# A planned attention and FFN kernel: denominator scaled to a constant of 1, clip free to run on GpSimd, new recorded order

## The chip, the cores and the metric

The kernel runs on one core of one Trainium2 chip. The metric is device microseconds of one execution. The three runs of the kernel before took 618.22, 619.12 and 624.07 us; the median is 619.12 us.

## The reference, cut to what matters

The first half is a gated linear recurrence over 768 time steps for 4 batches and 8 heads of 48 channels. The second half is an FFN of width 2048 whose activation is a rational function.

```python
mag = np.sqrt(a_re * a_re + a_im * a_im)
scale = np.minimum(mag, 0.999) / (mag + 1e-06)          # the clip
for t in range(S):                                       # S_re, S_im: complex 48 x 48 state of each head
    new_re = ar * S_re - ai * S_im
    new_im = ar * S_im + ai * S_re
    S_re, S_im = (new_re + kv, new_im)
    y[:, :, t] = np.einsum('bhd,bhde->bhe', q[:, :, t], S_re)
h = x @ w_in                                             # x: 3072 x 384, w_in: 384 x 2048
P = a[0] + a[1] * h + a[2] * h2 + a[3] * h3
Q = 1.0 + np.abs(b[0]) * np.abs(h) + np.abs(b[1]) * h2   # the denominator
g = P / (Q + 1e-06)
return (g @ w_out).astype(np.float32)
```

## The kernel before, in words

The recurrence is computed in chunks of 128 time steps. A unit is one chunk of one batch; there are 24 units, and two units make a pair (12 pairs). For each unit `norm` squares and clips the gates, takes reciprocal square roots and runs a running product along time; `angle` and `trig` give the phase as a sine and a cosine; `outer` turns q and k by them and copies the result by six DMAs into the buffer HQ; `attn` runs the matmuls of the unit on TensorE: transposes (line 566), scores (line 579, two groups of four heads, each into one of two PSUM banks), the masked scores and the state times the values (line 599), and the state update (line 604). For every pair `ffn` then runs 8 steps of 512 columns. One step is two slices of the hidden width: the first matmul into `ph` (line 632), a chain of elementwise operations, and the second matmul into `po` (line 649). The first two pairs use whole float32 weights, and the other ten pairs use weights and activations split into a high and a low part, so that three cheaper products stand for one. `weights` builds the float32 weights at the start from the raw words that are loaded, and `split` makes the two parts.

The elementwise chain of a step, by engine: ScalarE (ACT) takes |h| from `ph` into A1 and a square with a bias into A3; squares A1 with a bias into A2; takes the reciprocal square root of A2 plus a constant into the PSUM tile `z`; and squares `z`. VectorE (DVE) multiplies `ph` into A3, then makes two steps that refine the reciprocal in `z`, and the product that becomes `g`; in the split pairs `g` is also cut into two parts by ACT or DVE and by DVE or GpSimd (POOL). There are 96 steps.

```python
scal(AF.Square, 512, t2, t1, (A1, "co"), (A2,), more=93, bias=bh)         # line 677
scal(ROOT, 512, tz, t2, (A2, "co"), (z,), bias=q0, more=93)               # line 680, q0 = ks, a column
stt(512, t2, t2, q0, tz, (A2, z, "co"), (A2,))                            # line 682
```

No scheduler of the compiler sets the order. Every operation is put into a plan with the engines that may run it and an estimate of its time. The string ORDER holds a recorded order of all operations and the engine of each, and the operations are issued in that order, so each engine works its own part of the list in turn. The estimates in the plan play no part in an execution as long as ORDER fits the list.

SyncE (SP) issues nearly all DMAs in the same recorded order, and a DMA that waits for its data holds back the ones behind it.

Of the kernel before, what the change touches and what calls it, by code (L numbers as in the profile page):

```python
# [217 lines left out]
def act(n, psum=False):  # L218
# [11 lines left out]
    "=L&f?mR=^o2K7;K+$OfS4wqEwa9LYPDz)3IpUFa^eN(E)My(aH;lV@BT%Ar9s!KIXZ)*{Cw3=z$yb)YIubsrt^hud6F}hO*uv>$$%!0D=FP$vq)yi5O!TpVO"  # L230
    "f;+(8*8nvrR1HQr_cY2R+X?cRv9^qcI9C4`Y$CVhez1~rCwO1Vhz1I6c}Xx+ZIs@XzXOwOs-y(Q*hbDkU81)nUe`*lJ|tswxm*h-)m)VIrT(ci<pVR{-qZR{"
    "QSeZ(hV!nb%Dv!dSuZI}*+cS~+|)14t6mkykx}$yu%<~k8Qj&n&gDSaykxy;zOiLwgjr>;>wCd$NtfYz!)&l2QcF7M5-BUK%|1KasCPp*Nl#PJt|zNO+Fte$"
    "$pEb?bE*6|ljD8Cv}FZa=MA8Djhxa>a_|eLb`AG@PCY->4!Tf2mhw(&@T9hoW6Z@OiF6hO2HHgZf?XHLn`XV;8>}ELo#VmBop_xupOIr4J$gr~OK**KyXVab"
    "&f)q){oIVO2|V?boB=iUWsFSJzd^uh-5{@P2%TvH(ms(z`Ums3QVvT~Enq@cyOX`Yw7mPCjdF$uM>uPODeQ97d}vEclB&*=Bf*%Eq~IIW+tAC}5-%0pA)X^O"
    "Wf)ae9qH88Nm{|Z<V}~yq`y`N%hRN?4w21r(%kTpOl_Ma{iUTg)8E;5r)~_^4XLC3iRqk%$$xYJ75obXzAT$T;KQ=VUF4<nyf8r<xuZZ|W7iJgqPp9Y?ylq6"
    "P-bL~zD=x|ZbR>FDJ4;$_Eo83itGVc<6Dzs6SNdqE~2uf<tVe7s=FkS3igtCceVG0CNn{f>@UG%ruLBy+EAJidnZtKP<Odwy>(RZS=pldLC0!6F5R@BOk=f6"
    ";A|PY>~^nuPit>^1U{%E&&Uqb&wc`af~;Ar#l-%a+u!R*T_)=oNpw4TF<f6`*FD-*o^tznBe>d2oi=)VV3dh)$4{n{y{l>TY?u3kcUOypKTDi!(huE%u*?{F"
# [713 lines left out]
```

## Time and profile before

| | |
|---|---|
| median of three runs | 619.12 us |
| the profiled execution: its time, and the span from first to last instruction | 621.97 us, 620.2 us |
| TensorE (PE) busy | 552.5 us, 89% of the span |
| VectorE (DVE) busy | 561.2 us, 90% |
| ScalarE (ACT) busy | 515.7 us, 83% |
| GpSimd (POOL) busy | 278.9 us, 45% |
| mean granted TensorE clock | 0.984 of full speed |

The profile is one execution, and the sums are made against it. Busy time of an engine is the union of its instructions, so two instructions that overlap in the pipeline are counted once; a group's mean duration counts the overlap. Matmul ends are modelled, so a short pause between two matmuls can hide inside a busy TensorE.

### The profile page before, as it was taken

The numbers are of one execution on the slowest core, as the hardware profiler recorded it, in microseconds if no ns is written. First come the engines' busy times: TensorE is split into PE (matmuls) and PEld (weight loads), VectorE is DVE, ScalarE is ACT, GpSimd is POOL, SyncE is SP. The second block draws the span as 40 slices with busy tenths as digits, with TensorE's granted clock in tenths as the row PEclk, the third lists the DMA queues.
The fourth block names the chain that finished last, engine by engine and source line by source line (L and its number), as shares of the span: only waits on it lengthen the run. The fifth ranks groups of instructions, "written<-read, shape, count | busy, mean of one in ns | idle before, by whom it ended". The sixth has DMA issues, their size and how long they took to land.

```text
span 620.2 us, 16732 instructions
## 1 busy us (share of the span) xinstructions
PE 552.5 (89%) x6786; PEld 506.8 (82%) x6786; DVE 561.2 (90%) x984; ACT 515.7 (83%) x886; POOL 278.9 (45%) x244
## 2 busy tenths in 40 slices
PE   0048868899999999999999999899999999999994
PEld 0036645687679999999999999899999999999993
DVE  8999999799999999998999998989899989986893
ACT  7746999789799999999899899789888798677780
POOL 1012452457478587565465885663755400211110
PEclk9999988899999999999999999899999999999998
DMA  8699227474524470461461541553543604130001
GB/s 298 214 255 305 90 77 144 80 144 104 116 57 121 95 158 15 105 163 27 77 175 53 132 97 32 98 127 97 95 113 78 150 2 88 38 102 2 1 1 57
DMA packets 39109, 64.87 MB, mean 105 GB/s; under 512 B 4464, under 2 KB 26224, under 8 KB 39024
## 3 DMA queue, kind: packets, MB, share of 16 engines
q1 hardware_dynamic: 37872, 62.67, 40.6%
q10 hardware_dynamic: 1152, 1.05, 0.9%
q8 instruction: 55, 0.90, 0.7%
q14 instruction: 30, 0.25, 0.1%
HBM read 40.11 MB, written 4.72 MB: 72 GB/s over the span
## 4 chain that ended last, share of the span: by engine, by line
PE 64%; DVE 20%; DMA 7%; ACT 4%; issue 3%; SPq 1%; POOL 0%; ACTq 0%; DVEq 0%; POOLq 0%
PE po L649 26%; PE ph L632 26%; PE bank L599 5%; PE bank L579 4%; DVE A L338 4%; DMA HQ<-Q 3%; DVE T L338 3%; DVE MM L338 2%; PE bank L566 2%; PE bank L604 1%; DVE wo L338 1%; DVE z L338 1%; DVE wi L338 1%; ACT A L350 1%; DMA AA<-in_aa 1%
## 5 line engine op out<-in xcount | busy, mean ns | idle before, releaser
L649 PE MATMUL po<-wh,g 128*128 128x384 f32 x640 | 181.4, 340 | 0.0
L632 PE MATMUL ph<-xT,wiH 128*128 128x256 f32 x960 | 161.7, 287 | 0.3 <-DVE A L338 0.3
L649 PE MATMUL po<-wo,g 128*128 128x384 f32 x428 | 148.2, 387 | 2.1 <-DVE g L338 2.0
L338 DVE SCALAR_TENSOR_TENSOR A<-A,co,z 128x512 f32<-128x512 f32 x176 | 130.5, 742 | 20.1 <-ACT z L350 17.7
L632 PEld LDWEIGHTS ph<-xT,wiH 128*128 128x128 f32 x960 | 136.7, 191 | 2.5 <-DVE A L338 0.7
L632 PE MATMUL ph<-xT,wi 128*128 128x256 f32 x632 | 128.3, 322 | 7.2 <-DVE A L338 4.1
L338 POOL TENSOR_TENSOR g<-A,g 128x512 fp32r<-128x512 f32 x48 | 65.1, 1364 | 137.0 <-ACT z L350 40.2
L649 PEld LDWEIGHTS po<-wh,g 128*128 128x128 f32 x640 | 117.2, 188 | 2.1 <-issue 0.6
L632 PEld LDWEIGHTS ph<-xT,wi 128*128 128x128 f32 x632 | 103.0, 195 | 17.1 <-DVE A L338 4.1
L649 PEld LDWEIGHTS po<-wo,g 128*128 128x128 f32 x428 | 80.4, 191 | 15.1 <-DVE g L338 2.4
L350 ACT ACTIVATE z<-A,co 128x512 f32<-128x512 f32 x96 | 66.3, 690 | 21.8 <-DVE A L338 18.5
L338 DVE SCALAR_TENSOR_TENSOR A<-A,co,ph 128x512 f32<-128x512 f32 x96 | 71.0, 739 | 9.4 <-ACT A L350 9.4
L350 ACT ACTIVATE A<-A,co 128x512 f32<-128x512 f32 x96 | 69.1, 720 | 1.4 <-DVE g L338 0.4
L350 ACT ACTIVATE A<-ph,co 128x512 f32<-128x512 f32 x96 | 65.2, 680 | 3.3 <-DVE A L338 1.7
L338 DVE SCALAR_TENSOR_TENSOR z<-A,z 128x512 f32<-128x512 f32 x96 | 66.3, 691 | 1.8
L350 ACT ACTIVATE A<-ph 128x512 f32<-128x512 f32 x96 | 56.7, 591 | 11.7 <-PE ph L632 9.2
L566 PE MATMUL bank<-ident,HQ 96*128 96x96 f32 x160 | 19.5, 260 | 44.1 <-DVE wh L338 36.2
L350 ACT ACTIVATE z<-z 128x512 f32<-128x512 f32 x96 | 56.2, 585 | 1.5
L566 PEld LDWEIGHTS bank<-ident,HQ 96*128 96x128 f32 x160 | 17.1, 147 | 47.1 <-issue 42.3
L579 PEld LDWEIGHTS bank<-HQ 96*32 96x32 f32 x1536 | 32.8, 117 | 10.3 <-issue 3.0
L338 DVE TENSOR_TENSOR ST<-bank,cmask 128x512 f32<-128x512 f32 x48 | 32.0, 683 | 8.8 <-PE bank L579 8.3
L579 PE MATMUL bank<-HQ 96*32 96x32 f32 (+3 forms) x1536 | 37.8, 248 | 1.4 <-ACT kT L344 1.1
(175 smaller groups left out, 957.7 us busy)
## 6 DMA issues: line engine op xcount, KB each, us to landing
HQ<-Q SPq DMA_DIRECT2D x136, 128.0 KB, 5.1
AA<-in_aa SPq DMA_DIRECT2D x23, 384.0 KB, 3.6
QK<-in_qk SPq DMA_DIRECT2D x23, 384.0 KB, 4.9
V<-in_v SPq DMA_DIRECT2D x24, 352.0 KB, 4.7
g<-in_w_out SPq DMA_DIRECT2D x8, 384.0 KB, 5.2
wh<-in_w_in SPq DMA_DIRECT2D x6, 512.0 KB, 4.3
wh<-in_w_out SPq DMA_DIRECT2D x8, 384.0 KB, 4.3
g<-in_w_in SPq DMA_DIRECT2D x6, 512.0 KB, 5.2
```

Of the source, the lines that this page charges most:

```text
L338: call = lambda e: getattr(e, kind)(*map(real, args), **{k: real(x) for k, x in kw.items()})
L350: plan.op(dict(ACT=(act(n, psum) + more, lambda e: e.activation(o(), i(), f, **kw))), r, w)
L566: e.transpose(pt[:, i].bitcast(F32R), hq[0:96, 4 * g + i, 1, :], ident[0:96, 0:96])
L579: e.matmul(pst[m:m + 32, i, 32 * y:C], hf[:, 4 * g + i, 1, 32 * y:32 * y + 32], hf[:, 4 * g + i, 0, 32 * y:C], start=True, stop=True)
L599: e.matmul(py[32 * y:32 * y + 32, min(j, 2), :], l, sts[h // 4][:, h % 4, :] if q is None else hf[:, h, 0, :], start=q is None and j == 0, ...
L604: e.matmul(pd[y:y + 32, h], kT[:, h, y:y + 32], V[:, n:n + D], start=True, stop=True)
L632: e.matmul(ph[:, x * T:x * T + T].rearrange("p (h t) -> p h t", h=nb), wt[f // 4 * NJ + j][:, f % 4 * P:f % 4 * P + P], xT[:, x0:x0 + nb, ...
L649: e.matmul(po[b][:, 0:DM], gg[:, b * C:b * C + C], wt[:, 0:DM], start=(f == 0 and n == 0), stop=(f == NFF - 1 and n == len(prods) - 1))
```

## The change: what it does, and the diff

A factor `al` is computed once from the coefficients, by the reciprocal square root of the old constant `ks` and one refining step. The square of A1 takes `al` as a scale beside its bias, so that the constant to be added to A2 becomes 1. The reciprocal square root and the first refining step then take the number 1.0 where they took a column of `co`. The clip of `norm` may be placed on DVE or POOL. The string ORDER is another one; its characters are left out below. The estimates of `scores` and `values` in the plan differ, and one threshold in the test of the coefficients.

```diff
 ORDER = (
...
-    ra, rb, c2, c2h, c1, c1s, c0, bh, ks, sc, tmp = (co[:, i:i + 1] for i in range(11))
+    ra, rb, c2, c2h, c1, c1s, c0, bh, ks, sc, tmp, al = (co[:, i:i + 1] for i in range(12))
...
+    def scales(e):
+        e.tensor_tensor(tmp, al, al, ALU.mult)
+        e.tensor_tensor(tmp, tmp, ks, ALU.mult)
+        e.tensor_scalar(tmp, tmp, -0.5, 1.5, ALU.mult, ALU.add)
+        e.tensor_tensor(al, al, tmp, ALU.mult)
+        e.tensor_tensor(bh, bh, al, ALU.mult)
         e.tensor_tensor(sc, av[:, 3:4], rb, ALU.mult)
-        e.tensor_scalar(sc, sc, -1.0, None, ALU.mult)
-
-    plan.op(dict(DVE=(1500, ratios)), ("ab",), ("co",), port=True)
+        e.tensor_tensor(tmp, al, al, ALU.mult)
+        e.scalar_tensor_tensor(sc, sc, -1.0, tmp, ALU.mult, ALU.mult)
+
+    plan.op(dict(DVE=(1200, ratios)), ("ab",), ("co",), port=True)
+    scal(ROOT, 1, lambda: al, lambda: ks, ("co",), ("co",))
+    plan.op(dict(DVE=(700, scales)), ("ab", "co"), ("co",), port=True)
...
-        vec("tensor_scalar", W, lambda: MM.t, lambda: SQ[:, 1], CLIP2, None, ALU.min, two=False, r=(s1,), w=(MM,))
+        vec("tensor_scalar", W, lambda: MM.t, lambda: SQ[:, 1], CLIP2, None, ALU.min, two=False, r=(s1,), w=(MM,), eng=DP)
...
-            pe(565, scores, u.hq, (pst,))
+            pe(584, scores, u.hq, (pst,))
...
-        pe((1980 if c else 1010) + (0 if last else 600), values, (V, *sts, *u.hq, ("St", bb), *(() if last else (kT,))),
+        pe((1769 if c else 885) + (0 if last else 676), values, (V, *sts, *u.hq, ("St", bb), *(() if last else (kT,))),
...
-                scal(AF.Square, 512, t2, t1, (A1, "co"), (A2,), more=93, bias=bh)
-                k1, k0, q0 = c1s, c0, ks
+                scal(AF.Square, 512, t2, t1, (A1, "co"), (A2,), more=186, bias=bh, scale=al)
+                k1, k0, q0 = c1s, c0, 1.0
...
-            scal(ROOT, 512, tz, t2, (A2, "co"), (z,), bias=q0, more=93)
+            scal(ROOT, 512, tz, t2, (A2,), (z,), bias=q0)
...
-            stt(512, t2, t2, q0, tz, (A2, z, "co"), (A2,))
+            stt(512, t2, t2, q0, tz, (A2, z), (A2,), more=0)
```

Where instructions stand is shown at two places. The first is TensorE early in the split FFN, at the scores of the seventh unit (HQ0). `bank0` and `bank1` are the two PSUM banks of the attention, `ph` is the result of the first FFN matmul, `wiH` and `wi` are the high and the low part of its weights. Before, the last two rows of one group of scores, a slice of the FFN and the first row of the other group:

```order
L579 MATMUL bank1_106<-HQ0_92 32x64
L579 MATMUL bank1_106<-HQ0_92 32x32
L632 MATMUL ph_1805<-xT_1536,wiH3_850 128x256
L632 MATMUL ph_1805<-xT_1536,wiH4_1119 128x256
L632 MATMUL ph_1805<-xT_1536,wiH5_737 128x256
L632 MATMUL ph_1805<-xT_1536,wi2_1265 128x256
L632 MATMUL ph_1805<-xT_1536,wi3_1309 128x256
L632 MATMUL ph_1805<-xT_1536,wi4_1315 128x256
L632 MATMUL ph_1805<-xT_1536,wiH3_850 128x256
L632 MATMUL ph_1805<-xT_1536,wiH4_1119 128x256
L632 MATMUL ph_1805<-xT_1536,wiH5_737 128x256
L579 MATMUL bank0_105<-HQ0_92 32x128
```

Now, at the scores of the same unit:

```order
L589 MATMUL bank1_106<-HQ0_92 32x128
L589 MATMUL bank1_106<-HQ0_92 32x96
L589 MATMUL bank1_106<-HQ0_92 32x64
L589 MATMUL bank1_106<-HQ0_92 32x32
L589 MATMUL bank0_105<-HQ0_92 32x128
L589 MATMUL bank0_105<-HQ0_92 32x96
L589 MATMUL bank0_105<-HQ0_92 32x64
L589 MATMUL bank0_105<-HQ0_92 32x32
```

The two groups of scores now follow each other without FFN matmuls between them. Counted over the whole order, other matmuls stand between the two groups in 13 of the 24 units before (the 6th, 7th, 10th, 11th, 14th to 17th, 19th to 23rd) and in 1 now (the 22nd).

The second place is DVE in the first pair's FFN, while the weights are still being built. A row that writes `z` ends one FFN step. `wi` and `wo` are weights being built, `Q` are the turned q and k that the six DMAs of a unit read, `SQ`, `MM`, `T` and `RU` are tiles of `norm` and `outer`. Before, between the fourth and the fifth row that writes `z`:

```order
L338 SCALAR_TENSOR_TENSOR z<-A_747,z 128x512
L338 SCALAR_TENSOR_TENSOR g<-A_744,co,z 128x512
L338 COPY ncar<-MM 128x3
L338 TENSOR_REDUCE fl<-T 128x2
L338 TENSOR_SCALAR MM<-SQ 128x384
L338 SCALAR_TENSOR_TENSOR A_787<-A_787,co,ph 128x512
L338 SCALAR_TENSOR_TENSOR A_771<-A_771,co,z 128x512
L338 SCALAR_TENSOR_TENSOR z<-A_771,z 128x512
```

Now the end of the same piece; seven rows stand ahead of these and behind the fourth row that writes `z`:

```order
L338 SCALAR_TENSOR_TENSOR wo_746<-wh_643,wo_746 128x384
L338 SCALAR_TENSOR_TENSOR MM<-MM,ncar,SQ 128x128
L338 SCALAR_TENSOR_TENSOR RU<-Z,RU 128x3x128
L338 SCALAR_TENSOR_TENSOR MM<-MM,ncar,SQ 128x128
L338 TENSOR_TENSOR RU<-MM,RU 128x3x128
L338 SCALAR_TENSOR_TENSOR MM<-MM,ncar,SQ 128x128
L338 TENSOR_TENSOR T<-T,thc 128x6
L338 TENSOR_TENSOR Q<-QK,CO 128x768
L338 TENSOR_TENSOR Q<-QK,T 128x768
L338 SCALAR_TENSOR_TENSOR A_806<-A_806,z 128x512
L338 SCALAR_TENSOR_TENSOR z<-A_806,z 128x512
```

The piece has 7 rows behind the fourth write of `z` before and 18 now. The two rows that make `Q` of the third unit stand in the fifth step now; before they stand in the seventh. The row that writes A from A and `z` has no `co` any more.

## Rows read from the trace of the kernel before

**Rows 1.** Busy time by stretch: us, busy (instructions) of each engine, granted clock, DMA.

```profile
56.00:172.00 116.00, 102.61 (x970) 76.17 (x971) 109.43 (x199) 100.94 (x174) 56.40 (x51) 0.96 0.51 119
172.00:611.00 439.00, 436.01 (x5511) 418.41 (x5510) 396.40 (x653) 377.62 (x649) 215.49 (x174) 1.00 0.35 81
```

**Rows 2.** The two longest waits of PE, 172 to 612 us: total us, times, longest.

```profile
PE bank L566 <- DMA HQ<-Q: 1.6, 1, 1.6
PE bank L566 <- DVE St L338: 0.9, 2, 0.8
```

**Rows 3.** The chain of waits, in order of time: start us, us, what.

```profile
172.94 2.15 PE ph L632 x18
175.09 1.29 PE po L649 x4
...
216.18 6.47 PE ph L632 x54
...
282.55 1.89 PE bank L599 x64
...
285.11 2.35 PE ph L632 x18
...
288.51 0.61 PE bank L566 x8
...
579.48 3.12 PE po L649 x18
...
599.53 10.94 PE po L649 x63
```

**Rows 4.** Instructions of PE in order of time, scores in one piece: start us, us.

```profile
204.25 0.34 PE L649 MATMUL po<-wh,g 128*128 128x384 f32 x1
204.52 1.33 PE L579 MATMUL bank<-HQ 96*32 96x128 f32 x64
205.78 0.45 PE L649 MATMUL po<-wh,g 128*128 128x384 f32 x1
206.07 0.33 PE L649 MATMUL po<-wo,g 128*128 128x384 f32 x1
```

**Rows 5.** The same view, one group of scores between FFN matmuls.

```profile
243.71 0.52 PE L632 MATMUL ph<-xT,wiH 128*128 128x256 f32 x3
244.15 0.77 PE L579 MATMUL bank<-HQ 96*32 96x128 f32 x32
244.85 0.62 PE L632 MATMUL ph<-xT,wiH 128*128 128x256 f32 x3
245.31 0.52 PE L632 MATMUL ph<-xT,wi 128*128 128x256 f32 x3
```

**Rows 6.** Groups of instructions: count, busy us, mean ns, idle before them.

```profile
L338 DVE SCALAR_TENSOR_TENSOR A<-A,co,z 128x512 f32<-128x512 f32 x176 | 130.5, 742 | 20.1 <-ACT z L350 17.7
L350 ACT ACTIVATE A<-A,co 128x512 f32<-128x512 f32 x96 | 69.1, 720 | 1.4 <-DVE g L338 0.4
L338 DVE SCALAR_TENSOR_TENSOR z<-A,z 128x512 f32<-128x512 f32 x96 | 66.3, 691 | 1.8
L350 ACT ACTIVATE z<-A,co 128x512 f32<-128x512 f32 x96 | 66.3, 690 | 21.8 <-DVE A L338 18.5 <-DVE g L338 1.5 <-DVE T L338 0.8
L692 ACT ACTIVATE g<-A 128x512 fp32r<-128x512 f32 x49 | 30.3, 625 | 2.9 <-PE po L649 2.0 <-DVE A L338 0.9
L338 DVE TENSOR_SCALAR MM<-SQ 128x384 f32<-128x384 f32 x23 | 10.7, 464 | 0.1
L338 POOL TENSOR_SCALAR SQ<-SQ 128x384 f32<-128x384 f32 x3 | 1.6, 522 | 0.0
```

**Rows 7.** Instructions of DVE in order of time, while POOL is idle.

```profile
7.39 0.36 DVE L338 TENSOR_SCALAR MM<-SQ 128x384 f32<-128x384 f32 x1
```

**Rows 8.** Waits of PE and of DVE, 56 to 172 us: total us, times, longest.

```profile
PE bank L566 <- DMA HQ<-Q: 3.0, 1, 3.0
DVE ST L338 <- PE bank L579: 2.8, 2, 2.4
```

More of the change, by code (lines that the diff above doesn't have):

```diff
@@ new lines @@
+    "lH?!#M~zIBdAdhi$v*8UuSr|=q=FRlO)UQgfAS<+Zs{GZDTR7i+UP~CBd0V`3N%bs$|U_=D@p?2#Y%)+(6Z84{?yBQOUp^7Ow-NMTo=h4J;xj8Oon?oQj4wJ"
+    "&;>G1OY|OzmBrFkD@i4JUKVLUf7aC!$#;`wnU0XMQdbVEnkjy)jArLNov%Y|Q#Vr2=u|u1UoVepYw0Xicw>$%;QgcezPzDLWPsc&XW9Rf7HcCptrK(tdAv!?"
+    "lUY})cgq>=9QAGZ%kGv=;k3D0P5Mfr?DgUU6=az??9UYPG!<NZEs`Gki44^$vPIhIE@{Ayec7dw?d!JaOL9=BYjv3<L&)?a?IUrly;}xJRq3U3r4#SGBl-G<"
+    "J|sR-WSUCu3CYsurHL6Y<6OQb$ZdT^zarjVx`IsZlU%JV$zea<sUTCR_*8jZhHFyTkAZ?fr?6djZtCMyVxp|qfm9`$%HIl|pW`jM6Cstndn1pRgh^>2!8;YG"
@@ new lines @@
+    "?3Dy!rMBeBI(<$WnOqkxw|P3=jCGM9psd`Ci7ukV=Bk@vX1Vej<~gmYm*hg=E-zNj2i}&cQeMhwSudUMZ)uFAnu=mwkybZjizX(HIaAMjPM7OHU?E9f(CXe*"
+    "9k16llirr-C>^J>WC0Pz%9)tTZmblURqS%Fbkr=#XLlcr_!^}z*$KY&?qZjb(og4^?(TpLHS^s9A}vF0=S!MdqOnE8^>uv<)C}YEM>zu4K9+rfObO@=T}Yj)"
+    "%TnpA8S<eX)@JepwI8Do*%U{nbb7XorJk`;XeVErDdUN9jUHsp3XP_ZSrX}`1?I^uDNEd*ZRmQjZ)M&bqtl3Xv23JEs;_~V|C*D2yj<3Lbh^4s)MAtGPm<|c"
+    "Uw+q>-V1?-GK7;W$wh4_{lIsBKFflb2_Sr|x#~{?11B{_zZNTlIbp3C;nLZAwLR~z)zjKdv!#sGk`o#ZazE3)62{z316{4837_S~*g<|RdB9}5H`$}5>FHF*"
@@ new lines @@
+    "OOYN3WXm9Lpw^QA1n&1%Yd=|SzIQpM&`*>!%>~z4>{(6@$Y9pwnA?75Spo{X66+x?0K297gACAI?IGJuZ?{}iIqgIKXZhxD{me9Rb-{l+{T(V_>o|!sPrJ97"
+    "!do#5+$jBzyhDW(v<q1u&~186p3!gUYF~K-7T8F|W5~C^UFw&GYi7tu%{2{OroG$$O&U_q2jy?gGSQOa0vg4+&%y|6wJuYUl+^m{2%;ayB)`w3y<k7{-__TN"
+    "<$3vDi@;2=R+X#ztuB{Rv(f*aIvoX#k@RA&US*y?_vdSxybUAW(Cxa?X8HSdfV{4QWRs>4)jrMBAxvFsGI|gkUbIvFoqE~~bgd-b?(*NFzinZhzFNgz@vo7;"
+    "m6v6<egO}Tk)|+Sp}eHQC;y^?LnT8;%RBlLOmLFf{}BE;BX<H7y!~d0AIW*1bhFz+Kcz_vJJb)Cmh}96ovnFNUw6wL6X!PTO`WPonBZ1&*_`ux%0~DogG^Ux"
@@ new lines @@
+    "dHAIlC@j&*a7{J(n<m|1?H9oESLOp)Y^<*3X&G4$hU(jR_c~o@DGPO(T+vOS{u`L~PrU?lCM7jJTdG%dv<BDiw6px}+JT9#Y&*KHGE7#pW}I#Sk#)&=nXU)X"
+    "@7eZ#7dp63&cTnWd(A_x3Y@i8`kL7;MSj*)vRDK&+$Hnv3coy9?Cq+_yV^^ln9gSMoq5U?YG0G-g84L(CPcqkztlBSQ&yPHZk2u`OLZ+BiUNHrwT|gn^t6t)"
+    "E#R+IaIx78ay`r%=TXDuD8P2}g?krXs}0^RlV7s^#Lqy#Qs~ZAeHZK$nsxpdSUFh?Q7xgem%(ytU25977o`tcR-K=Q%Qh6zH?>`fK4Me-A)v4VXGF0gSL4hT"
+    "rtJWAeMDZR=FRNipsgI(?E=3vWb%iiI!{S=JxAT{ljlIjO?}a>_k-AY(SGDVBd5XZ3=l9J{JpIg=xT|MrB=g1XE|wX+q(?*iqX^XMO%q-J%~R5+Go@CFF@^C"
@@ new lines @@
+    "-KBNxQU3>RV-Ndd*=L^qk$CJ(S9s#ln4zwjSBENO=mmX3lI0WTs4DZAr(NY^Eo(X#MaqBmRid0m9~;R+xtramF?)Hsk<Wg1j=u*apW(DHSszoUC|ldf(~=dF"
+    "TC|ajOW}uWX0_X(Tl7gZw<%iP9%c7ns2r2$52H%o!CG15lmp_PwcGuHF!W|Kn10uWqnp}st|j{Zj`_+TZ|k@n<~}eGMpS)p7r!JfK08di!!hsaWg<?;4?Gk4"
+    "Zl@kM#-+ji*TKaSyTcFYTpecL^Sj9wB5Th#vsmp>rPHjh!ycYIB)^g89$lnC4qwc)9Ki?7;<FBsHstRlnWc@XM+VQj(ysw>hz>{NiY}RZLCiwdoYCJj)mC>4"
+    "^bK|$kDdhGL;$DM!0vJDnWI_oWHue&54QhiexfB_`k6<Vpr7?T8ax=}Jt?o-Hq63NqC8Jco(Z(}c54r_&$eU&zo1_W;oO?MQOM-f$5~~=)YtJkll9*`|Ac)8"
@@ new lines @@
+    "$>+K#P}5rvn?5CvNjm%z%sSY!(|Qp8`irb56G@6(F~@bMzl^Fz$?cdvMV(l)RWt1SelC5RO#I_;RhvvpmxaH{G|^0Gj%n`tODeHMlW7(Dy@yE~uTP_Pdttj7"
+    "?54US$Y5aPS8XdhKu$ofpa$={5uk21Pflo>UFX-uooo-e$u%%wn)J4t{Rk@e3R<SRKjc1hn6~y*ye0i@gX(tEZFURHn9j2XvRv<y1}O9(dyl_KeqolH@joAS"
+    "U7>%W_S1<YfHqYk&S;q+C(Qf2+t?oT%W&Sup(&eS+Q~8h6`d(}h-CzPG6z;z4I^ZN_seijcXB<9gZPrFY+y|Xuv~~{og%tBaKsgS%U0aiBB~10NPB%o-q!QD"
+    "=ES7>XZPq<sR4=(>#0Ds*o#`uS7}Y&yKG0llwBSKX^Y^5pG~Z*!P%2=MRP!t^IO6z<vDu?-e{HH#3A;w9sI|c*I()TEc|Q=KQ#sihfE_EAwiGc$#wzvN6lOp"
@@ new lines @@
+    "&x$nW=A?eFgUNplUUHkxH7~hBQw{bircc%2xmW2^w0xHse)b8eM<ng(N<6AntV?v8tTX%lKGMo2`$Kt>OxzXu%%XBbq#aIaCJLKFz7=7-aK713ub(2yEpnU="
+    "l<NHwBM-=oP?wWIZmG7AhwV(ivUJjH8|4~H1-r+erJF!~a9*yV%2CoqqHU&&gs+2)*8x}54;4GDpTUB=O_)QyLk!SKK4s!=Fuf^sW2<^zN2Vczn)IYH3ph7V"
+    "*VqdFc<OM1JIYb*Zfm>$Rn^xBCVqon(<!o>t}P?8{&?Au=y4&jjKYcBB${lny_FkC3iEXbe|=Jq2gFNde&@17RolTW!b=6H!VMI?FPKl2@sdJKTf^na*K)nX"
+    "8pkc=3VV&xi8?m6wVz547lW{T-Dg_3FzGKZnp9j$hSs&M+*a-cGw}SSFy$%TZCCpvm~0ORS%wbvX2KSkU+^5q(D(xFZ$82coCXo!(6>Xp_b4c>4tl$zW4D-)"
@@ L270 @@
+    "3s$BE+Sr8ECA@tC2lz**62Whh<PVs3KNY%2y({CFmCpv~o5ut;m;YDSBPjJfOy4=GU(H=nHHq##Yol0`YudZ(+!Uf<f@`qKpS*pRTeJsC8n7aUn4&@o6AcId"
+    "st+?WH#jqoCwp*t`E<UTi{{iDeA^tQ+lnVW2}X8vlPu8SZz=O(caJ^tna)zZZkoD+&>X}ug(Xa38LCo|eWOs3>L~IlZq=7VU8@!P4d?%U(|HH}EiiYvf9QB5"
+    "-aSHsH3^s78vN@?S$tzz&I$f0hYtvF##{J=F#ePYJ^eqdrFae"
 )
@@ L874, in coefs_ok @@
         e.tensor_tensor(cf[:, 4:5], babs[:, 0:1], babs[:, 0:1], ALU.mult)
[L875 removed]
+        e.scalar_tensor_tensor(cf[:, 7:8], babs[:, 1:2], 3.75, cf[:, 4:5], ALU.mult, ALU.is_ge)
         e.tensor_scalar(cf[:, 8:9], cf[:, 3:4], 2.0 ** -20, None, ALU.is_ge)
```

58 lines of the change are left out of this document (13 added, 45 removed).

## The prediction

> **What bounds the kernel now.** I first read the busy time by stretch [rows 1]. Cut at 172 us, where the split FFN begins, the run has two faces. From 56 to 172 us DVE is busy 109.43 of 116 us, PE only 102.61, and the granted clock is 0.96: DVE carries the building of the weights, the preparation of units and the FFN's elementwise chain at once, and PE waits for it. From 172 to 611 us PE is busy 436.01 of 439 us at full clock, DVE 396.40, ACT 377.62. The waits of PE in that stretch agree: the two longest sum to 2.5 us [rows 2]. So a microsecond taken from DVE, ACT or POOL counts fully only ahead of 172 us; behind it only what shortens PE's own work counts, and what removes PE's few stalls.
>
> Busy PE can hide short pauses, so I add up the matmuls from the first split slice at 172.94 us to the end of the last one at 599.53 + 10.94 = 610.47 us, 437.5 us [rows 3]. First FFN matmuls: 54 take 6.47 us, 0.120 each, and 160 slices of 9 make 172.5 us. Second FFN matmuls: 18 take 3.12 us, 0.173 each, and 160 times 6 make 166.4. Five slices of the second whole pair are still to do at 1.29: 6.5. Scores of 18 units: one unit in a piece costs, from the end of the matmul before it (204.25 + 0.17) to the moment from which FFN matmuls keep their pace again (206.07 - 0.17), 1.47 us [rows 4]; 18 make 26.5. Values and states: 285.11 - 282.55 = 2.56 us, and 0.20 more because the 18 matmuls behind them take 2.35 in place of 2.15; 14 units make 38.6, and four without a state update, at 1.89 + 0.20, make 8.4. Transposes, 0.61 and about 0.14 of toll, 14 units: 10.5. With 3.5 us for scores that are cut in two (below) the sum is 432.9. About 4.6 us are left for waits of every kind; that is all that a better order can win from stalls there.
>
> **The change part by part.**
>
> *Scores in one piece.* One group of scores between FFN matmuls costs, reckoned the same way, (245.31 - 0.36) - (243.71 + 0.36) = 0.88 us [rows 5]. Two such groups are 1.76 us, one piece is 1.47, so each cut costs 0.29 us, which lies between matmuls of the engine that sets the end. Of the 13 units that are cut before, 12 lie in the split stretch (12 times 0.29 is the 3.5 above); one is left now. Eleven cuts less: **-3.2 us**. The price can be gone if PE then waits for the masked scores (DVE) ahead of the values; in the new order FFN work stands between them, as before. Ends: 0 and -3.2.
>
> *DVE in the chain.* The first refining step drops its column. The group with a column takes 742 ns, the one with a number 691 [rows 6]: 51 ns, 96 times, 4.9 us of DVE.
>
> *The clip.* Counted over the order, 15 of 23 clips in this group go from DVE to POOL. DVE loses 15 times 464 ns, 7.0 us; POOL gains 15 times about 522 ns, the nearest row of the same shape, 7.8 us [rows 6]. Other operations move too (T, RU, T plus CO and kT to DVE, Q to POOL); all moves and the chain's 4.9 us together, each at the mean of its group, leave DVE some 6 us lower and POOL some 5 higher. The clip is not free of charge: on DVE it took 0.36 us at 7.39 us, when POOL did nothing [rows 7], and 464 ns on average, so the two engines hinder each other.
> The Trainium skill, SBUF — State Buffer, section Who interferes with whom, says that a GpSimd instruction that reads SBUF and a DVE instruction with two SBUF inputs exclude each other, and that whoever comes second waits for the whole of the first. By that rule the 15 clips could cost DVE up to 7.8 us again, more than the 7.0 they free, and the sum below would lose the gain that I allow for stalls, ending at about 614 us.
>
> *ACT.* The reciprocal root loses its column and the square of A1 gets a second one. A square of A with one column takes 720 ns, a copy from the same kind of tile without one 625: 95 ns per column [rows 6]. So the root goes from 690 to about 595, 9.1 us over 96. No row has an instruction with two columns; the second one costs between nothing and another 95. I take 95, the same row, which makes ACT's sum 0; the other end is -9.1 us on ACT, off the path.
>
> *The start.* The new ops on the coefficients are eight one-column DVE operations where two stood, a few tenths of a microsecond beside loads, and one tiny ACT operation; nothing waits for them before the first FFN step. Four HQ copies of the first two units go from ACT's queue to SP's. SP holds weight loads behind them, but these wait for their staging buffers, which DVE empties; I take 0.
>
> *DVE's order before 172 us.* Summing the rows of the order with each group's duration back to back, DVE's work up to the ninth row that writes z is 123.8 us in both orders, and up to the 17th, the first split step, 165.8 before and 166.4 now. What differs is the way there: up to the fifth it is 84.8 before and 91.8 now. The shown piece is most of it: 18 rows in place of 7, and 11 rows at 109.43/199 = 0.55 us are 6 us [rows 1]. It brings the third unit's Q forward by two steps. Before, that unit came late: PE waited 3.0 us for its HQ copy and DVE 2.8 us in turn for scores [rows 8]. Ends: -5.8 us (both waits go) and +7 (the early steps are late and nothing makes up for it). DVE sets the pace here and its work is equal at the ninth and the 17th step, so I expect only part of its idle time back: **-2**.
>
> *Stalls behind 172 us.* With DVE some 6 us lower in all and Q made with more lead, about half of the 4.6 us: **-2.3**; ends 0 and -4.6.
>
> The tail is unchanged: the last reductions, two column pieces of output and their DMAs. The last first-FFN matmul is now followed by 14 slices of second matmuls in place of 11, so the last chain has more cover, not less.
>
> Sum: -3.2 - 2 - 2.3 = -7.5 us. The profiled execution's own 621.97 would become 614.5. It stands 2.85 above the median of 619.12, so the forecast for the median is **611.6 us**, taken as 612.
>
> **The rivals.**
> *The elementwise engines were the pace after all.* For it: DVE waits 18 us in all for the root in z, and ACT as long for DVE [rows 6], so the chain is tight everywhere. Against it: PE's busy time. Then all of DVE's 6.6 idle us before 172, all 4.6 behind it and the 3.2 go: -14.4, 605 us. Chance 0.12.
> *The first pair starves (slower).* Place: FFN steps two to five of the first pair on PE, which wait for DVE's product with ph. DVE reaches the fifth step 7 us later. PE has only 116 - 102.61 = 13.4 us of slack in the stretch [rows 1], and the clock is not full there: 0.96 means about 9 us at 1.2 instead of 2.4 GHz. If the lateness carries through, the time is 619.1 + 7 - 3.2 = 623, and one more fall of the clock, 2 us, gives 625. It decides once the first split slice starts more than 3.2 us after 172.94, that is behind 176. For it: the row counts. Against: equal work at the ninth and 17th steps, and the earlier Q. Chance 0.18.
> *The merge and the moves do nothing.* Scores in one piece make PE wait for the masked scores, and new short stalls take the place of old ones; DVE and ACT get lighter where PE is the bound. Then 617 to 620 us. Chance 0.15.
>
> **How the numbers follow.** Forecast 0.55, and the rivals as given. A measurement of this kernel can tell about 1% from no change, 6.2 us, so faster by that is below 612.9. The forecast at 612, with its terms' ends some 4 us either way, is below that in about two thirds of its cases: 0.36, and with the first rival 0.48. Within 1%: the rest of the forecast 0.19, the third rival 0.15, and a third of the second 0.06: 0.40. Slower: 0.12. For the range: the low end 604 takes in the first rival; the high end 621 takes in the third and the milder half of the second.
>
> **What would show it.** The chain of waits should still run through PE's lines 642 and 659 behind 172 us, with scores as rows of 64 at 1.3 us and hardly any of 32. The first split slice should start at 169 to 173 us; behind 176 the slower rival is right. DVE's group A from A and z should stand near 691 ns, the root near 595, the square of A1 near 815. PE's busy time from there to its last reduction should be about 3 us less than before. If that stretch is as long as before with its cuts gone, stalls took the gain; if it is more than 8 us shorter, my account of hidden waits was wrong.

## The result, and the profile after

The changed kernel takes 623.73 us (median; 620.44 to 626.91) against 619.79 for the kernel before, run beside it: ratio 1.0066, 95% interval 1.0046 to 1.0086. It is slower by 4 us, where 612 was forecast, and outside the range of 604 to 621. Its profiled execution took 623.88 us with a span of 622.2; the one of before took 621.97 and 620.2, so the two traces differ by only 1.9 of the 4 us. Below, one run of e12 (714.91 us) and one of e13 (631.10) stand apart from the others of their kernel; the ratios leave them out.

Busy time by stretch, changed kernel; the columns are those of [rows 1] (the engines are PE, PEld, which is PE's weight loads, DVE, ACT and POOL), and the long stretch is cut in three here:

```profile
56.00:172.00 116.00, 101.99 (x1035) 76.36 (x1028) 106.75 (x201) 101.27 (x174) 61.86 (x55) 0.94 0.45 120
172.00:240.00 68.00, 63.77 (x800) 57.55 (x802) 63.50 (x103) 59.97 (x108) 48.04 (x40) 1.00 0.52 114
240.00:330.00 90.00, 88.77 (x1211) 85.92 (x1200) 84.98 (x145) 80.92 (x140) 53.99 (x46) 1.00 0.42 98
330.00:611.00 281.00, 278.49 (x3502) 270.82 (x3503) 246.68 (x407) 234.45 (x400) 128.57 (x96) 1.00 0.31 73
```

The kernel before, same view, the second stretch:

```profile
172.00:240.00 68.00, 68.00 (x920) 62.90 (x919) 66.63 (x113) 64.48 (x115) 52.53 (x43) 1.00 0.41 98
```

This is the row that the prediction lacked. Before, PE never paused in those 68 us, and DVE was busy for 66.63 of them, 98%: more than ahead of 172 us. Now PE stands for 4.2 us there, and DVE for 4.5. From 330 us on PE is as busy as before (278.49 us against 278.34).

The waits of PE behind 172 us, changed kernel (for [rows 2]):

```profile
PE bank L609 <- DVE ST L338: 2.5, 2, 2.1
PE ph L642 <- DVE A L338: 1.8, 4, 0.8
PE ph L642 <- ACT xT L350: 1.4, 1, 1.4
PE bank L609 <- DMA V<-in_v: 1.0, 1, 1.0
```

The longest one, traced back over three engines in order of time (in brackets the idle time ahead, and who ended it). PE:

```profile
198.77 0.34 PE L659 MATMUL po<-wh,g 128*128 128x384 f32 x1
201.20 1.08 PE L609 MATMUL bank<-ST,V 128*32 128x128 f32 x32 [2.09 <-DVE ST L338]
```

DVE, same kernel:

```profile
195.84 0.74 DVE L338 SCALAR_TENSOR_TENSOR A<-A,co,z 128x512 f32<-128x512 f32 x1
198.33 1.62 DVE L338 TENSOR_TENSOR wo<-wo,wh 128x384 fp32r<-128x384 f32 x1 [1.75 <-POOL wo L338]
199.87 1.27 DVE L338 TENSOR_TENSOR ST<-bank,cmask 128x512 f32<-128x512 f32 x2
201.66 0.54 DVE L338 TENSOR_TENSOR wo<-wo,wh 128x384 fp32r<-128x384 f32 x1
```

POOL, same kernel:

```profile
195.35 1.84 POOL L338 TENSOR_TENSOR QK<-QK,RU 128x768 f32<-128x768 f32 x1 [3.01 <-DMA QK<-in_qk]
197.13 0.19 POOL L338 COPY ncar<-MM 128x3 f32<-128x3 f32 x1
197.28 1.02 POOL L338 TENSOR_TENSOR wo<-wo,wh 128x384 fp32r<-128x384 f32 x1
```

POOL waits 3.01 us for a late load; a part of wo stands behind that product; DVE waits 1.75 us for it and then takes 1.62 us for an operation that takes 0.54 at 201.66 us; the masked scores ST stand behind that; PE waits 2.09 us.

Groups of instructions, changed kernel (for [rows 6]):

```profile
L338 DVE SCALAR_TENSOR_TENSOR A<-A,z 128x512 f32<-128x512 f32 x96 | 65.2, 679 | 25.4 <-ACT z L350 25.3
L350 ACT ACTIVATE z<-A 128x512 f32<-128x512 f32 x96 | 57.5, 599 | 30.3 <-DVE A L338 29.0 <-DVE g L338 0.9
L350 ACT ACTIVATE A<-A,co 128x512 f32<-128x512 f32 x96 | 77.9, 812 | 2.9 <-POOL g L338 1.6
L338 POOL TENSOR_SCALAR MM<-SQ 128x384 f32<-128x384 f32 x15 | 18.0, 1201 | 6.1 <-DVE SQ L338 5.4
```

Scores in one piece, instructions of PE in order of time (for [rows 4]):

```profile
231.42 0.34 PE L659 MATMUL po<-wh,g 128*128 128x384 f32 x1
231.69 1.33 PE L589 MATMUL bank<-HQ 96*32 96x128 f32 x64
232.96 0.64 PE L642 MATMUL ph<-xT,wiH 128*128 128x256 f32 x3
233.43 0.52 PE L642 MATMUL ph<-xT,wi 128*128 128x256 f32 x3
```

Reckoned as in the prediction, this unit costs 232.96 - (231.42 + 0.17) and 0.11 us of slower matmuls behind it, 1.48 us; 1.47 was used (the rows of [rows 4] give 1.48 as well).

When FFN work is reached, from the first matmul of a step in each trace (us; the forms of [rows 3]):

| trace | first FFN matmul | step 16, first split | step 28 | last reduction ends | step 28 to there |
|---|---|---|---|---|---|
| before | 56.3 | 172.5 | 228.9 | 611.0 | 382.1 |
| changed | 61.7 | 174.1 | 234.1 | 612.9 | 378.8 |

Both traces record the same matmuls ahead of step 16, and the same ahead of step 28. The changed kernel is 5.2 us behind at step 28, and wins 3.3 us from there on. From step 16 to the last reduction it takes 438.8 us, before 438.5. That is the prediction's own sign that stalls took the gain: the stretch is as long as before, though the scores in it are no longer cut.

### The profile page after: what moved, and what is told of

It reads as the page before. It is cut to its first block, busy times and chain, and to the rows that moved or that the text cites. A ratio compares the mean times of both kernels' runs of the same rounds, so it can differ in the third digit from the quotient of the medians.

```text
span 622.2 us, 16731 instructions
## 1 busy us (share of the span) xinstructions
PE 546.5 (88%) x6786; PEld 502.1 (81%) x6786; DVE 556.0 (89%) x986; ACT 511.8 (82%) x880; POOL 304.1 (49%) x255
## 4 chain that ended last, share of the span: by engine, by line
PE 51%; DVE 24%; ACT 14%; issue 4%; DMA 4%; POOL 1%; SPq 1%; DVEq 0%; ACTq 0%; POOLq 0%
PE ph L642 21%; PE po L659 20%; DVE A L338 5%; PE bank L609 4%; ACT A L350 4%; PE bank L589 3%; DVE T L338 3%; ACT z L350 3%; DVE z L338 2%; DVE wo L338 2%; DVE wi L338 2%; DVE MM L338 2%; DMA V<-in_v 2%; DVE ST L338 1%; DVE SQ L338 1%
## 5 line engine op out<-in xcount | busy, mean ns | idle before, releaser
L338 POOL TENSOR_TENSOR g<-A,g 128x512 fp32r<-128x512 f32 x52 | 71.4, 1379 | 106.1 <-ACT g L702 60.5
L338 DVE SCALAR_TENSOR_TENSOR A<-A,z 128x512 f32<-128x512 f32 x96 | 65.2, 679 | 25.4 <-ACT z L350 25.3
L350 ACT ACTIVATE z<-A 128x512 f32<-128x512 f32 x96 | 57.5, 599 | 30.3 <-DVE A L338 29.0
L350 ACT ACTIVATE A<-A,co 128x512 f32<-128x512 f32 x96 | 77.9, 812 | 2.9 <-POOL g L338 1.6
L338 DVE SCALAR_TENSOR_TENSOR A<-A,co,z 128x512 f32<-128x512 f32 x80 | 59.5, 743 | 1.7
L576 PE MATMUL bank<-ident,HQ 96*128 96x96 f32 x160 | 18.0, 249 | 41.8 <-DVE wh L338 37.2
L338 POOL TENSOR_TENSOR Q<-QK,T 128x768 f32<-128x768 f32 x14 | 29.7, 2120 | 24.5 <-DVE QK L338 13.6
L338 POOL TENSOR_TENSOR QK<-QK,RU 128x768 f32<-128x768 f32 x14 | 29.0, 2074 | 20.7 <-DMA QK<-in_qk 8.1
```

The costliest lines, as they stand in the source:

```text
L338: call = lambda e: getattr(e, kind)(*map(real, args), **{k: real(x) for k, x in kw.items()})
L350: plan.op(dict(ACT=(act(n, psum) + more, lambda e: e.activation(o(), i(), f, **kw))), r, w)
L576: e.transpose(pt[:, i].bitcast(F32R), hq[0:96, 4 * g + i, 1, :], ident[0:96, 0:96])
```

## The experiments

Ratios are to the kernel before, run beside each kernel on the same chip, with 95% intervals; 0.1% is 0.6 us. Where an edit is one of the order, its diff names the engine, and the entries in their new and old sequence.

**One part of the change at a time.** e1: the order of before, formula new. e2: the changed order with its engines, formula old (one line of it is shown). e3: the changed kernel, clips on DVE. e4: the kernel before, only the two groups of scores of each unit put together; on DVE one masked score and one copy follow them to a new place.

```diff
 e1  ORDER of before, and its two new entries (al, scales)
 e2 -scal(ROOT, 512, tz, t2, (A2,), (z,), bias=q0)      # changed
    +scal(ROOT, 512, tz, t2, (A2, "co"), (z,), bias=q0, more=93)
 e3 -POOL: 15 of MM<-SQ
    +DVE:  15 of MM<-SQ, in the same places
 e4 -PE: scores bank1 | FFN matmuls | scores bank0   (13 units)
    +PE: scores bank1 | scores bank0
```

> The new formula and the immediate constant, in the order of the kernel before (the two new small operations put in at the start, the clip on DVE everywhere). If the order is what made the changed kernel slower, this one is not slower than before: DVE loses 96 times 63 ns behind a TensorE that sets the pace, so 617 to 620 us, ratio 0.995 to 1.000. If the formula itself costs (the second column on ACT's square stands ahead of the root in every step), it is slower than before by most of the 0.7%: 622 to 624 us.

> The order and the engines of the changed kernel, clips on GpSimd included, with the old formula (the two small operations left out). If the order is the cause: as slow as the changed kernel or slower, since DVE is 6 us heavier again: 623 to 628 us. If the formula is the cause: 618 to 620 us.

> The changed kernel with its 15 GpSimd clips put back on DVE at the same places of the order, nothing else changed. If GpSimd's clips cost (they hold back what DVE does with two inputs, or lengthen the way from the squares to the running product): faster than the changed kernel, 620 to 622 us. If only the order matters: 623 to 626 us, DVE 7 us heavier.

> The kernel before with one thing moved: in the 13 units whose two groups of scores had FFN matmuls between them the groups now follow each other, as in the changed kernel. By the price of the prediction, 0.29 us for a cut, 12 of them behind 172 us: 3 to 3.5 us faster, 616 to 617 us, and TensorE's busy time behind 172 us 3.5 us less. If the values then wait for the masked scores, the price is given back: 619 to 620 us, with new waits of the matmuls on ST.

| run | median us | ratio |
|---|---|---|
| e1 new formula, old order | 621.58 | 1.0012 [0.9981, 1.0043] |
| e2 new order, old formula | 628.92 | 1.0153 [1.0112, 1.0193] |
| e3 changed, clips on DVE | 633.53 | 1.0237 [1.0198, 1.0275] |
| e4 before, scores in one piece | 617.19 | 0.9961 [0.9937, 0.9986] |

The loss is that of the order. With the old formula it costs 1.5%, 9 us. The formula wins nothing in the old order (e1 was expected at 617 to 620), and 0.9%, 5.4 us, in the new one, where it frees 96 times 63 ns (742 less 679), 6.0 us of DVE. The clips on POOL win 1.7%, 10.6 us; e3 is slower than either theory had it. Back on DVE the clips take longer than the 464 ns of before:

```profile
L338 DVE TENSOR_SCALAR MM<-SQ 128x384 f32<-128x384 f32 x23 | 15.4, 668 | 0.7 <-POOL SQ L338 0.7
```

DVE is busy for 568.7 us in e3's trace, for 565.1 in e2's and for 556.0 in the changed kernel's. Against 12.7 and 9.1 us of DVE stand 10.6 and 5.4 us of time: in the new order most of DVE's load counts. The merge alone wins 2.4 us: 0.19 us for each of 13 cuts (0.07 to 0.30), 0.29 was forecast.

**Where in the order.** e5 takes the chain above apart by one move on POOL. e6 and e7 splice the two orders at FFN step 28, e9 and e10 at step 16, all with the new formula. e8 puts the parts into the old order.

```diff
 e5 -POOL: QK<-QK,RU | ncar<-MM | wo<-wo,wh
    +POOL: wo<-wo,wh | QK<-QK,RU | ncar<-MM
 e6  old order to step 28 | changed order        e7  changed to step 28 | old
 e9  old order to step 16 | changed order        e10 changed to step 16 | old
 e8  old order, scores of each unit together, new formula, the 15 clips on POOL
```

> The changed kernel with one operation moved: on GpSimd the low part of one block of the second FFN weights (1.02 us at 197.28 us in its trace) stands ahead of the product with QK, which waits 3.0 us there for a late load, and no longer behind it. Theory (the new order loses on one chain near 200 us: late QK load, GpSimd behind it, DVE 1.75 us waiting for the wo part, the masked scores late, TensorE 2.1 us waiting): the 2.1 us wait of TensorE for ST at 201 us goes, 621 to 622 us. Rival (DVE's total work sets the pace of the new order): DVE's 1.75 us come back as well, but other short waits take them; 623.7, no change. Rival (GpSimd's queue as a whole is too full there): the next piece is late in its place, 623 to 625.

> The new formula; the order, engines included, is that of the kernel before until the first matmul of FFN step 28 (about 229 us), and that of the changed kernel for everything that is left. Theory (all of the loss lies between 172 and 240 us; measured in finished TensorE work the changed kernel falls 5.4 us behind there and wins about 2 us over the old order behind it): 617 to 620 us, below the old order with the new formula (621.6). Rival (the loss is spread over the whole order, since DVE is the pace everywhere in it): about 622.6, half way.

> The reverse splice: the order of the changed kernel until the first matmul of FFN step 28 and that of the kernel before for the rest, with the new formula. Theory (loss between 172 and 240 us, nothing won behind it): 625 to 627 us, slower than the changed kernel. Rival (spread): about 622.6.

> The order of the kernel before with three things of the change put into it: the scores of every unit in one piece, the new formula, and the same 15 clips on GpSimd. Theory (in the old order TensorE is the bound, so only what shortens TensorE's own work counts): as the merge alone, 616 to 618 us. Rival (lighter DVE and ACT count in any order, as they do in the new one, 5 us for the formula and 10 for the clips): 605 to 612 us. Rival (clips on GpSimd hold back GpSimd's other work in an order not made for them): 620 us or more.

> New formula; the order of the kernel before until the first matmul of FFN step 16 (the first split slice, about 172 us), that of the changed kernel for the rest. Two theories on the loss ahead of step 28. Theory A (the loss is made by the order of steps 16 to 28 itself, where DVE is busy 97% of the time, with the late QK load and the two short waits for xT): 622 to 624 us, near the changed kernel. Theory B (it is handed over at step 16: the new order arrives there with more work of DVE and GpSimd left undone): 618 to 620 us, near the splice at step 28 (618.84).

> The reverse splice at step 16, new formula. It has 12 units with cut scores. Theory A (loss made in steps 16 to 28): 621 to 623 us, near the old order with the new formula (621.58). Theory B (handed over at step 16): 625 to 627, near the reverse splice at step 28 (626.91).

| run | median us | ratio | step 28 at |
|---|---|---|---|
| e5 part of wo ahead of QK | 622.99 | 1.0036 [1.0011, 1.0060] | 237.6 |
| e6 old to 28, then new | 618.84 | 0.9975 [0.9958, 0.9992] | 229.6 |
| e7 new to 28, then old | 626.91 | 1.0084 [1.0059, 1.0110] | 238.9 |
| e8 merge, formula, clips in old order | 618.62 | 0.9973 [0.9949, 0.9997] | 232.4 |
| e9 old to 16, then new | 621.14 | 1.0015 [0.9996, 1.0033] | 229.8 |
| e10 new to 16, then old | 629.11 | 1.0133 [1.0111, 1.0156] | 238.3 |

The kernels compared here differ by at most two units with cut scores, some 0.4 us. The order ahead of step 28 is the loss: it costs 0.9%, 5.6 us, with the new rest (changed against e6), and 0.7% with the old one (e7 against e1). Within it neither theory of e9 and e10 is enough: e9 lies between the two, and e10 is slower than both. The start up to step 16 costs 0.5% with the new continuation (changed against e9), 3.2 us, and 1.2% with the old (e10 against e1), 7.5 us; steps 16 to 28 of the new order cost 0.4% behind the old start (e9 against e6) and win 0.5% behind the new one (e7 against e10). Start and continuation fit each other. e8 shows that in the old order, where PE does not pause behind 172 us, formula and clips add nothing to the merge. e5 gained 0.3%, its interval overlapping that of the changed kernel; in its trace the 2.1 us wait for ST is gone.

e10 tells what the new start hands over. Waits of PE, 172 to 240 us:

```profile
PE bank L576 <- DMA HQ<-Q: 5.9, 1, 5.9
PE ph L642 <- ACT xT L350: 0.9, 1, 0.9
```

The seventh unit is late. Its second Q, the product with T, left POOL and stands at the end of a step on DVE. On SyncE, the first copy that needs this Q holds back the copies of the other Q, which POOL had done at 167.11 us. The load of QK of the eighth unit stands there too, but it would have to wait in any case: the kernel has one buffer for QK, and this product reads it until 172.44 us. DVE in order of time, changed kernel:

```profile
171.19 1.25 DVE L338 TENSOR_TENSOR Q<-QK,T 128x768 f32<-128x768 f32 x1
```

POOL, same kernel:

```profile
165.29 1.82 POOL L338 TENSOR_TENSOR Q<-QK,CO 128x768 f32<-128x768 f32 x1 [5.18 <-ACT CO L522]
```

SyncE, same kernel:

```profile
172.50 0.55 SPq L332 DMA_DIRECT2D HQ<-Q  x1
173.14 0.54 SPq L332 DMA_DIRECT2D QK<-in_qk  x1
173.74 1.87 SPq L332 DMA_DIRECT2D HQ<-Q  x3
```

And before, POOL, which made this product first and the one with CO behind it:

```profile
159.86 1.82 POOL L338 TENSOR_TENSOR Q<-QK,T 128x768 f32<-128x768 f32 x1 [0.83 <-ACT T L512]
161.64 1.93 POOL L338 TENSOR_TENSOR Q<-QK,CO 128x768 f32<-128x768 f32 x1
```

SyncE, before, where the load leaves as soon as both products are done (161.64 + 1.93 = 163.57 us):

```profile
163.60 0.33 SPq L332 DMA_DIRECT2D QK<-in_qk  x1
```

**The late unit and the clips.** e11: as e6, with the scores together in the old part too. e12: only the 5 clips ahead of step 28 back on DVE. e13: the second Q of the seventh unit on POOL, behind the first. e14: e13, its last two copies on SyncE no longer behind one of the eighth unit, and the move of e5. e15: the splice of e10 with that Q and those copies early. e16: the kernel before with that Q late.

```diff
 e13 -DVE:  z | g | A<-A,co,ph | Q<-QK,T        (step 16)
     +POOL: Q<-QK,CO | Q<-QK,T
 e14 -SP: four HQ of unit 7 | V | V | HQ of unit 8 | two HQ of unit 7
     +SP: six HQ of unit 7 | V | V | HQ of unit 8
 e16 -POOL: Q | Q                               (kernel before)
     +DVE: behind eight more operations; SP: three HQ, QK<-in_qk follow it
```

> The version that by the runs so far should beat both kernels: new formula, old order with the scores of every unit in one piece until FFN step 28, the changed kernel's order for the rest. Against the splice at step 28 (618.84, 3 cuts) it has 2 cuts less, at 0.2 to 0.3 us each: 618 to 618.5 us. If the gains of the merge alone (2.4 us, 617.19) and of the later part of the new order (2.7 us) were two things that add up, 615 to 616.

> The changed kernel with the 5 clips that stand ahead of FFN step 28 on GpSimd back on DVE (2.3 us of DVE at 464 ns); the other 10 stay on GpSimd. All 15 back cost 9.8 us (633.53 against 623.73), of which the trace shows 6 between 172 and 240 us. Theory (DVE sets the pace ahead of step 28, and there alone): 628 to 632, more than half of the 9.8 by a third of the clips. Rival (DVE counts everywhere alike): 5 of 15, 627 us. Rival (its share of DVE time only): 2.3 us, 626.

> The changed kernel with one operation moved: the second Q of the seventh unit (1.25 us on DVE at 171.19 us) goes to GpSimd, right behind the first Q of that unit, which ends there at 167.1 us. The six copies of that unit and, queued behind the first of them on SyncE, the load of QK of the eighth unit (173.14 us, before 163.60) can then start some 3.5 us earlier. Theory (the loss ahead of step 28 comes from this late unit and what it holds back): 619 to 622 us. Rival (it does not matter for TensorE, since the new order uses the copies only at 187 us; DVE's sum is the pace): DVE loses 1.25 us, 622.5 to 623.7. Rival (GpSimd's Q slows DVE's two-input operations beside it): 624 or more.

> As the run before, and two more moves: the last two copies of the seventh unit no longer stand on SyncE behind the first copy of the eighth, and the part of wo at 197 us stands ahead of QK on GpSimd. Theory (three places, each a queue in which something ready stands behind something late): all of the loss ahead of step 28, near the old start with the new rest: 618 to 620.5 us. Rival (DVE's load is the pace, and where the pieces stand matters little): 622 to 623.5.

> The splice of the new order until step 16 with the old rest (629.11 us), with the seventh unit's second Q on GpSimd behind the first and its six copies together. The trace of that splice has one wait of TensorE of 5.9 us for a copy HQ of this unit at 178 us and a fall of the clock behind it. Theory (the new start hands over a late seventh unit, and that is its whole cost to the old rest): 621 to 624 us. Rival (it hands over work undone on DVE as well): 625 to 627.

> The kernel before, old formula, with that one operation moved the other way: the second Q of the seventh unit leaves GpSimd (161.6 us) and stands on DVE ten operations later (about 170 us); four entries of SyncE's queue that need it or stand behind it (three copies of that unit, the load of QK of the eighth) follow. Theory (this move alone makes the stall): TensorE waits about 4 us for HQ near 176 us and the eighth unit is late as well; 623 to 627 us. Rival (harmless): 619.5 to 621.

| run | median us | ratio |
|---|---|---|
| e11 merged old to 28, then new | 619.47 | 0.9991 [0.9970, 1.0011] |
| e12 five early clips on DVE | 630.19 | 1.0142 [1.0117, 1.0167] |
| e13 changed, that Q early | 623.67 | 1.0056 [1.0034, 1.0078] |
| e14 changed, three places | 624.80 | 1.0078 [1.0055, 1.0101] |
| e15 e10, that Q early | 624.60 | 1.0072 [1.0044, 1.0100] |
| e16 before, that Q late | 623.32 | 1.0056 [1.0037, 1.0076] |

The late Q is a real cost to the old order: alone it makes it 0.6% slower, 3.5 us (e16), and to make it early, with its two last copies, wins 0.6% in the splice (e10 to e15). How it costs e16 is shown in part only: about 4 us of waiting for HQ were expected, and its trace has one such wait, of 1.6 us. In the changed kernel it is worth nothing (e13; e14 is slower than either theory had it), as one rival said: its continuation asks for those copies later, at 187.46 us in place of 175.92. In e13 and e14 the first copy that needs the Q leaves at 171.88 and 172.26 us, with step 16 at 175.6 and 176.0: 2.2 us sooner against step 16 than in the changed kernel, where about 3.5 were expected. e11, expected at 618 to 618.5, is not told apart from e6. e12 agrees with DVE as the pace ahead of step 28: a third of the clips costs 0.8% of the 1.7%. PE's longest wait behind 172 us in e12:

```profile
PE ph L642 <- DVE A L338: 3.5, 1, 3.5
```

The wait of 3.5 us is for the product with ph, DVE's own row. In e14 the part of wo came in time, and ST was late all the same. DVE, e14:

```profile
199.47 1.97 DVE L338 TENSOR_TENSOR wo<-wo,wh 128x384 fp32r<-128x384 f32 x1
201.36 1.28 DVE L338 TENSOR_TENSOR ST<-bank,cmask 128x512 f32<-128x512 f32 x2
```

POOL, e14:

```profile
199.17 1.84 POOL L338 TENSOR_TENSOR T<-T,CO 128x768 f32<-128x768 f32 x1
```

The wait of 1.75 us had turned into an operation that takes 1.97 instead of 0.54 us beside POOL's. The Trainium skill, SBUF — State Buffer, section Who interferes with whom, says that a DVE operation with two inputs in SBUF and a GpSimd instruction that reads SBUF contend for a shared port pair, and that the one that issues second is blocked for the whole of the first; these rows agree, the DVE operation ending 0.43 us after POOL's.

**Two last moves on DVE.** e17: in the changed kernel the masked scores stand ahead of that wo. e18: four more early clips on POOL.

```diff
 e17 -DVE: wo<-wo,wh | ST | ST
     +DVE: ST | ST | wo<-wo,wh
 e18 -DVE:  MM<-SQ at steps 8, 10, 18, 21
     +POOL: MM<-SQ at steps 8, 10, 18, 21
```

> The changed kernel with one operation moved on DVE: the part of wo for which DVE waits 1.75 us at 196.6 us, and which then takes 1.62 us beside GpSimd, stands behind the two masked scores of the seventh unit instead of ahead of them. The scores end at 196.7 us, so the masked scores can be done at 198.2 and TensorE's 2.1 us wait at 199.1 us should go. Theory (this wait is lost time in the stretch where DVE sets the pace, about 2 of the 5 us): 621 to 622.5 us. Rival (the time comes back as another wait, as when the part of wo was put forward on GpSimd): 623 to 624.5.

> The changed kernel with the four clips that stand between FFN steps 8 and 21 on DVE (1.9 us of DVE) on GpSimd too; the four of the first units stay on DVE. Five clips of that part put back on DVE cost 6.5 us. Theory (DVE sets the pace ahead of step 28 in the new order, and GpSimd has room): 619 to 622 us. Rival (GpSimd's work and what it takes from DVE's two-input operations costs as much; its clip takes 1.17 us against 0.35 to 0.46 on DVE): 624 to 627.

e17 took 626.18 us, 1.0108 [1.0076, 1.0140]; e18 625.05 us, 1.0101 [1.0066, 1.0136]. e17 is slower than either theory had it. The wait for ST is gone, and a wait of the transposes for the state takes its place:

```profile
PE bank L576 <- DVE St L338: 1.7, 1, 1.7
```

e18 is as its rival said. DVE waits 3.0 us for the part of wo there, 1.75 in the changed kernel, and ST is later still:

```profile
PE bank L609 <- DVE ST L338: 3.2, 1, 3.2
```

Every trace with the new start lets PE work only 60.96 to 65.92 of the 68 us from 172 to 240; every one with the old start 66.39 to 68.00. From the first matmul of step 16 to that of step 28, ahead of which every trace records the same matmuls, it takes 58.6 to 66.8 us with the new start and 56.4 to 58.2 with the old one. In some traces part of that is the clock: granted from 172 to 240 us is 1.00 in the changed kernel, in e2, e5, e7, e14 and e15 and with every old start, but 0.97 in e3, e13 and e17, and 0.95 in e10, e12 and e18. 0.95 is 6.8 of 68 us at 1.2 GHz, work of 3.4 us at full clock. The row of e18:

```profile
172.00:240.00 68.00, 63.00 (x764) 57.43 (x765) 60.53 (x96) 55.94 (x100) 47.22 (x40) 0.95 0.46 106
```

Step 16 comes late as well, and one trace does not tell by how much. Five traces share the changed kernel's order up to there; with the old start and the new formula there are three:

| order up to step 16 | step 16, first split, us |
|---|---|
| changed: e10, changed, e17, e5, e7 | 173.3, 174.1, 178.3, 178.5, 178.7 |
| old, new formula: e9, e6, e1 | 171.8, 173.1, 173.9 |

## Why the prediction was wrong

- **The step that failed: "behind it only what shortens PE's own work counts", and with it the stalls behind 172 us (-2.3).** I took the stretch from 172 to 611 us as one. Its mean, DVE 396.40 of 439, hid the first 68 us, in which DVE is busy 98%, the weights are still being split and PE has work only because the start hands over in time. There PE stands for 4.2 us, where it stood for none before. By the splices the new order costs 5.6 us up to step 28 (changed against e6). Of these, 2.5 come with steps 16 to 28 (e9 against e6), where 2.3 were to be won, and 3.2 with the start; with the old rest the start costs 7.5 us and steps 16 to 28 give 3.0 back, so the two parts do not add up by themselves. e12 and e3 show that DVE's load is paid for in the new order.
- **DVE's order before 172 us (-2).** It measured +3.2 us with the new continuation (changed against e9) and +7.5 with the old one (e10 against e1). Equal sums of work at the ninth and 17th step were taken to mean equal progress. The sums were near enough, the progress was not: the 17th row that writes z ends on DVE at 186.1 to 190.9 us in the five traces with the changed start, and at 183.2 to 184.9 in the three with the old one. In the one pair of the result the late first steps (5.4 us at the first matmul) look made good by step 16 (1.6); the other traces do not bear that out. And a sum does not tell which unit's product is late: the prediction looked at the third unit's Q, and the seventh's went the other way, with the copies and the QK buffer that wait for it (e10, e15, e16).
- **Scores in one piece (-3.2).** Right in kind: -2.4 us in all for 13 cuts (e4), with the forecast price at the upper end of what e4 allows. From step 28 on the changed kernel does win 3.3 us; by the medians it is 2.7 (e6 against e1) and 3.2 (changed against e7).
- **The formula and the clip.** 679, 599 and 812 ns were forecast as 691, 595 and 815. The clip on POOL takes 1201 ns, not 522: 18.0 us in place of 7.8. What DVE's lighter load is worth was taken as nothing behind 172 us. That holds in the old order (e8, no better than e4), not in the new one (5.4 and 10.6 us). By the rule that I weighed (the Trainium skill, SBUF — State Buffer, Who interferes with whom), clips on POOL could have cost DVE as much as they free; e3 decides against that sum, though e14 shows the rule at work.
- **The rivals.** The starved first pair gave the time, 623, and part of the way. Its lateness carries through, but 3.2 us of it and not 7 (changed against e9); its mark, a first split slice behind 176 us, is missed in the changed kernel's trace (174.1) and reached in three of the five with that start. That its number is the measured one is luck: steps 16 to 28 make up the rest, and its sum had nothing there. "The merge and the moves do nothing" came near in kind too, with 617 to 620: new stalls took the gain, and more.

What stays open: which entries of the new start, besides the seventh unit's Q, the new continuation suffers from. Five repairs of single places (e5, e13, e14, e17, e18) took the named wait away, or moved it, and none won more than its uncertainty. That the next operation in DVE's row is late then is what e14 and e17 show; that this is so for all of the 5 us is an inference. What makes step 16 late by 3 us is not taken apart by any run. The lowest median is that of e4, the kernel before with its scores in one piece: 617.19 us, 0.9961 [0.9937, 0.9986]; e6 and e8 are not told apart from it.

## What to carry to other kernels

Cut the busy time finely before you call an engine the bound: a stretch of 68 us with a second engine at 98% can decide a change to an order that the mean of 439 us calls safe. When a recorded order changes, follow each unit's products to the queue that passes them on, what stands behind them there, and which buffer they free, not the sums of work. A start that varies by 5 us from one execution to the next wants more than one trace before a lateness is called made good. A gain on an engine off the path is worth nothing until an order makes that engine the pace; then it only pays back what the order has cost.

## What the runs showed of the hardware

- A two-input operation of DVE grew from 0.54 to 1.62 and 1.97 us beside an operation of POOL. The clip, with one input, is held as well: 0.36 us at 7.39 us with POOL idle [rows 7], and 1.96 us in e3, ending 0.22 us after POOL's operation. Waits of this kind raise e3's mean to 668 ns; moved to POOL the clips paid in the new order, although each takes 1201 ns there. DVE and POOL, e3:

```profile
316.84 1.96 DVE L338 TENSOR_SCALAR MM<-SQ 128x384 f32<-128x384 f32 x1
316.73 1.85 POOL L338 TENSOR_TENSOR QK<-QK,RU 128x768 f32<-128x768 f32 x1
```

- On POOL, two TENSOR_SCALAR groups of the same shape differ: the clip 1201 ns, the three of SQ 522 [rows 6].
- Each column less or more moves an ACT operation by some 92 ns: 690 to 599, 720 to 812.
- The clock: in e10 the stretch with the 5.9 us wait has a granted clock of 0.88, that is some 6.7 of 28 us at 1.2 GHz; in the changed kernel, with its 2.09 us wait, the stretch from 172 to 240 us stays at 1.00, 2.4 GHz; in e13, whose longest wait there is 2.1 us as well, it is 0.97. The row of e10:

```profile
172.00:200.00 28.00, 21.22 (x169) 17.03 (x168) 20.09 (x33) 19.60 (x38) 13.80 (x12) 0.88 0.48 113
```
